# Z of the last two modes as column-group partials, channel sums of a third pair beside the last weights, and six tiles finished singly

## The chip, the cores and the metric

The kernel runs on one core of one Trainium2 chip. The metric is device time in microseconds for one execution, the median of three runs. All times below are microseconds unless marked otherwise; positions are counted from the start of the profiled span.

## The reference

Linear attention (batch 8, 8 heads, 576 rows, head size 64) feeds a Fourier mixing layer of width 512. Of the 576 rows' spectrum the first 64 modes are kept, and each mode has its own complex 512 x 512 matrix:

```python
q_p, k_p = (phi(q), phi(k))                      # phi(x) = elu(x) + 1
kv = np.einsum('bhsd,bhse->bhde', k_p, v)
...
x = (num / den) ...                              # (8, 576, 512)
X = np.fft.rfft(x, axis=1)                       # the first 64 modes: Xr, Xi
Yr = np.einsum('bmd,mde->bme', Xr, w_r) - np.einsum('bmd,mde->bme', Xi, w_i)
Yi = np.einsum('bmd,mde->bme', Xr, w_i) + np.einsum('bmd,mde->bme', Xi, w_r)
y = np.fft.irfft(Y, n=S, axis=1)
u = x + y
return u + np.maximum(u @ w_ch, 0.0)
```

The weights w_r and w_i are 64 x 512 x 512 each, in float32 in HBM, and are read once.

## The kernel before

**Stages.** First the attention of the 8 batches and the forward transform, while the first weights load. Then 32 mode pairs: `mode_pair(p)` multiplies two modes by their weights as they land (`product`, L498), copies the result off (`evacuate`), picks it apart into a bank `yt` (`picks`, L521), and does slots of other work (`work_slot`), with filler products (`keep_warm`, L485, into the bank `zl`) where PE would idle. Weights are loaded by POOL's DMA queue, two pairs of buffers deep. Rows of the output are made of x, the inverse transform of Y, and the relu of E0 (= x @ w_ch and early modes) plus the inverse transform of Z = Y @ w_ch. Early and middle modes are folded into x and E0 during the mode pairs.

**The last pair.** `last_pair` handles modes 62 and 63. The last eight modes (`Y8`, 128 rows of mode x part x batch, 16 a mode) are turned in two steps. `ahead_rows` does the first six (rows 0 to 95, `RA` = 96): transposes to `ya_ps`, products with w_ch to `za_ps`, and two copies on ACT into `ahead` (the tile `rows_ahead`). Then follow the channel sums of tile pairs 0 and 1 (`channels`, L932: an identity product that puts E0 into an accumulator) with the middle modes' Z behind them (`first_rows`, L1024, 64 rows of the array); mode 62's products; its picks; and mode 63's products (`y_last`, L583), piece by piece as the weights land in five pieces, with a filler behind some of them. `ahead_gathers` sends the 96 ahead rows to their places in `YZ_all` by two DMAs, one of SP and one of POOL, which wait for the third piece from the end.

**The tail.** When mode 63's Y is copied (L591), all four chunks of `Y8` are transposed (L1102) and multiplied by w_ch in two halves of 256 columns (L1108, into `zl` and `z1l`); ACT and DVE copy Y to `last_y`, ACT copies both halves of Z to `last_z`. Output rows come in 36 tiles of 128 rows, done as 18 pairs. Pairs 0 to 3 (batches 0 and 1) take Y and Z straight from `last_y` and `last_z`, by `lead_sb`, the inverse transform's rows in the order of `Y8`. Later pairs read `YZ_all`, so they need the gathers; the rows of modes 62 and 63 go there by four POOL DMAs (L1118), Z first. For each tile: channel sum, Z product (`add_inverse` with half 1), relu on ACT in place, Y product (half 0), add on DVE to x, store by SP. Tile 0 has its Y added ahead (`y0`, L1115) and is finished by one DVE operation; three more tiles are finished singly (`add_one`, L1130); from pair 2 on `finish` (L965) adds two tiles in one DVE operation and stores 512 KB.

**Order.** `pin` keeps the written order on each engine. So PE does pair n's sums and Z product, then pair n-1's Y product. Accumulators lie in eight banks, two for a pair, given out in turn (`acc_pools`); `declare_no_dep` tells the tile framework that two banks of one tile do not depend on each other.

Of the kernel before, what the change touches and what calls it, by code (L numbers as in the profile page):

```python
# [10 lines left out]
F32 = mybir.dt.float32  # L11
# [22 lines left out]
def kernel(  # L34
# [10 lines left out]
    nc = tc.nc  # L45
# [428 lines left out]
    def w_get(p: int):  # L474
# [5 lines left out]
        return w_in[p]  # L480

    def keep_warm(n: int, cols: int = D):

        for _ in range(n):
            pin(nc.tensor.matmul(last_ps[0][:, 0:cols], id16, wch16[:, 0, 0:cols]))  # L485

# [31 lines left out]
    def picks(kk: int, st, n: int):  # L518
        for ec in range(NDC):
            pin(  # L520
                nc.tensor.matmul(  # L521
                    yt_ps[:, ec, kk % 8 : kk % 8 + n, :].rearrange("p m n -> p (m n)"),
                    st[:, ec * 128 : ec * 128 + 128],
                    pick_sb[:, 0 : n * 2 * B],
                )
            )

    def mode_pair(p: int):
        nonlocal yt_ps
        w = w_get(p)  # L530
        if p % 4 == 0:
            yt_ps = psW.tile([128, NDC, 8, 2 * B], F32, tag="yt", bufs=1, name=f"yt{p // 4}")
        P = psW.tile([128, D], F32, tag="P", bufs=2, name=f"P{p}")
        for dc in range(NDW):
            product(P, xz[p % 2][:, dc].rearrange("p h n -> p (h n)"), 32, w, dc, NDW)
        if p + 1 < LAST:
            set_diagonal(p + 1)
        st = evacuate(p, P)
        work_slot(p, "mid")
        if p == LAST - 1:  # L540
            keep_warm(3)
        picks(2 * p, st, 2)
        if p % 4 == 3:
            kk = 2 * p + 1
            if kk < NF:
                pin(nc.vector.tensor_copy(out=YE_T[:, :, kk - 7 : kk + 1, :], in_=yt_ps))
# [8 lines left out]
    def last_pair():  # L555
        xl = ystage.tile([128, NDL, 2 * B], BF16, name="xl")
        for h in range(2):
            src = xt_v[:, (2 * h + 1) * NDC : (2 * h + 2) * NDC, :, :, LAST]
            pin(
                nc.vector.tensor_copy(  # L560
                    out=xl[:, h * NDC : h * NDC + NDC], in_=src.rearrange("p c t b -> p c (t b)")
                )
            )
        w = w_get(LAST)
        kk = NM - 2
        ahead_rows()
        work_slot(LAST, "start")
        P = psW.tile([128, D], F32, tag="P", bufs=2, name=f"P{kk}")
# [6 lines left out]
        pin(nc.vector.tensor_copy(out=Y8[:, :, NA, :], in_=yt_ps[:, :, NA, :]))  # L575
        ahead_gathers()
        keep_warm(4)
        y_last = psW.tile([128, NDC, 2 * B], F32, tag="P", bufs=2, name="y_last")
        for piece in PIECES:
            for dc in range(piece.start, piece.stop):  # L580
                for ec in range(NDC):
                    pin(
                        nc.tensor.matmul(  # L583
                            y_last[:, ec, :], w[:, NDL + dc, ec * 128 : ec * 128 + 128], xl[:, dc, :],
                            start=(dc == 0 and ec == 0), stop=(dc == NDL - 1), skip_group_check=True,
                        )
                    )
# [3 lines left out]
        nc.vector.tensor_copy(out=Y8[:, :, NL - 1, :], in_=y_last)  # L591

# [7 lines left out]
    PSUM = bass.MemoryType.PSUM  # L600
    psW = tc.alloc_tile_pool(name="psW", bufs=1, space=PSUM, side="left")
    psB = tc.alloc_tile_pool(name="psB", bufs=1, space=PSUM, side="right")

# [14 lines left out]
    def late_modes(g: int, ps):  # L618
# [7 lines left out]
        for h, yl in enumerate(YL):  # L626
            rows = mode_rows(ps)[:, h * (NDC // 2) : h * (NDC // 2) + NDC // 2]
            for d in range(2):
                pin(nc.vector.tensor_copy(out=yl[:, :, d, :, g, :], in_=rows))

# [56 lines left out]

    last_ps = []

# [181 lines left out]
    def fold_lead(t: int):  # L871
# [13 lines left out]
        pin(nc.scalar.copy(out=e, in_=acc))  # L885

    def add_inverse(n: int, half: int, tiles_of=(0, 1)):

# [35 lines left out]
    def channels(n: int, tiles_of=(0, 1)):  # L924
        if n not in accs:
            accs[n] = acc_pools[n % 4 // 2].tile([128, 2, D], F32, tag="acc", bufs=2, name=f"acc{n}")
        for i in tiles_of:
# [46 lines left out]

    last_ps.append(psW.tile([128, D], F32, tag="zl", bufs=1, name="zl0"))
    made: set = set()
# [15 lines left out]
    for b in range(B):  # L992
        work.append(lambda b=b: form_z(b))
        work.append(lambda b=b: form_y(b))
        if b < N_LEAD:
            work += [lambda t=t: fold_lead(t) for t in range(b * NJJ, b * NJJ + NJJ)]
    n_form = len(work) - n_fold
    first_fold, first_form = NF // 2 - 1, NE // 2 - 1
# [21 lines left out]
    def first_rows(n: int):  # L1020
        for i, t in enumerate(pairs[n]):
# [22 lines left out]
    def ahead_rows():  # L1044

        pin(nc.vector.tensor_copy(out=Y8[:, :, 0:NA, :], in_=yt_ps[:, :, 0:NA, :]))
        ya_ps = psW.tile([128, NDC, 128], F16, tag="P", bufs=2, name="ya_ps")
        za_ps = psW.tile([128, D], F32, tag="P", bufs=2, name="za_ps")
        for ec in range(NDC):
# [34 lines left out]
    for n in range(N_PRE):  # L1084
# [3 lines left out]

    last = [
        sW.tile([128, D], F16, tag="x16w", bufs=2, name="last_y"),  # L1090
        sW.tile([128, NDC, 128], F16, tag="xTw", bufs=2, name="last_z").rearrange("p c r -> p (c r)"),
    ]
    z1_ps = psW.tile([128, NDC, 8, 2 * B], F32, tag="yt", bufs=1, name="z1l")
    y_ps = [
        psW.tile([128, NDC, 128], F16, tag="P", bufs=2, name=f"ypl{h}")[:, 0 : NDC // 2] for h in range(2)
    ]
    y0 = psW.tile([128, D], F32, tag="P", bufs=2, name="y0l")
    last_ps.append(z1_ps.rearrange("p c m n -> p (c m n)"))
    hw = D // 2
    COLS = [slice(h * hw, h * hw + hw) for h in range(2)]  # L1100
    for ec in range(NDC):
        pin(nc.tensor.transpose(y_ps[ec // 2][:, ec % 2, :], rows[ec], id16))  # L1102
    pin(nc.scalar.copy(out=last[0][:, COLS[0]], in_=y_ps[0].rearrange("p c r -> p (c r)")))
    pin(nc.vector.tensor_copy(out=last[0][:, COLS[1]], in_=y_ps[1].rearrange("p c r -> p (c r)")))
    for h in range(2):
        for ec in range(NDC):
            pin(
                nc.tensor.matmul(  # L1108
                    last_ps[h][:, 0:hw], rows[ec], wch16[:, ec, COLS[h]],
                    start=(ec == 0), stop=(ec == NDC - 1),  # L1110
                )
            )
        pin(nc.scalar.copy(out=last[1][:, COLS[h]], in_=last_ps[h][:, 0:hw]))
    pin(nc.tensor.matmul(y0, lead_sb[0][:, rows_of(0)], last[0]))
    pin(nc.vector.tensor_tensor(out=x_of(0), in0=y0, in1=x_of(0), op=ALU.add))  # L1115
    for z in (1, 0):
        for h in range(2):
            nc.gpsimd.dma_start(out=late_at(h, RA, 128 - RA)[:, :, z, :], in_=last[z][RA:128])  # L1118
    psW.release()
    acc_pools.append(  # L1120
        tc.alloc_tile_pool(name="psT1", bufs=1, space=PSUM, side="left", reuse_waits="tile")
    )
# [17 lines left out]
    on_bank(  # L1140
        0, {0},
        nc.vector.scalar_tensor_tensor(
            out=x_of(0), in0=accs[0][:, 0], scalar=0.0, in1=x_of(0), op0=ALU.max, op1=ALU.add
        ),
    )
    store(0, 1)
# [12 lines left out]
    for n in range(4, len(pairs)):  # L1159
# [3 lines left out]
    finish(len(pairs) - 1)  # L1163
    acc_pools[1].release()
    acc_pools[0].release()

# [28 lines left out]
```

## Time and profile before

| | |
|---|---|
| median of 3 runs (lowest, highest) | 419.69 (419.50, 419.86) |
| the profiled execution | 419.94 |
| its span | 418.2 |
| PE / DVE / ACT / POOL busy | 71% / 57% / 37% / 15% of the span |
| weights' queue (POOL) | 81.53 MB |
| SP's queue | 10.90 MB |
| last piece of weights lands | 387.3 |
| first store issued | 391.0 |
| last store issued, landed | 413.0, 417.3 |

The span runs from the first to the last instruction; the profiled execution is 1.7 longer than it. In rows of the timeline the columns are start, duration (of the whole group, from the first start to the last end), engine, line, operation, output<-inputs, shapes and count, and in brackets the idle time before and what ended it. In a row of a stretch, each engine has its busy time and count, then come the granted clock of TensorE, the DMA share and GB/s. A row of DMA issues ends with the size of each and the time from issue to landing. Rows of the chain are start, duration, and the work that the end hung on.

### The profile page before, as it was taken

To read this page: it belongs to the slowest core of one execution; us is meant where nothing else is said; L and a number is where in the kernel's file an instruction comes from. 1 tells how busy PE (TensorE), PEld (TensorE's weight loads), DVE (VectorE), ACT (ScalarE), POOL (GpSimd) and SP (SyncE) were. 2 spreads that over 40 slices of the span, in tenths; PEclk is the share of its full clock that TensorE was granted. 3 is DMA by queue.
4 is the path that set the end of the run, shared out by engine and by line. 5 is a ranking of instruction groups with operands and counts; after the bars stand their busy time and mean duration, and the time that the engine had idled before them with its cause. 6 is when DMAs were issued, how large, how long until landed. Compare 5 with 4: busy or idle time off the path is not lost.

```text
span 418.2 us, 6982 instructions
## 1 busy us (share of the span) xinstructions
PE 295.0 (71%) x2890; PEld 158.9 (38%) x2890; DVE 240.2 (57%) x533; ACT 153.2 (37%) x226; POOL 61.3 (15%) x110
## 2 busy tenths in 40 slices
PE   0279999999674455444435676978796967998992
PEld 0167777777411222212122232333342422453431
DVE  4779879995437474455536453564454534522794
ACT  4667767954200001000000233334352522331682
POOL 6222222300020111111111111111111111130200
PEclk9999999989755655556665589999897988899997
DMA  8999999999999999999999999999999999998698
GB/s 216 212 212 214 211 219 205 222 215 220 212 215 218 213 221 212 216 217 216 218 216 215 219 212 216 218 215 217 216 215 218 215 215 219 215 210 172 210 401 344
DMA packets 16564, 92.86 MB, mean 222 GB/s; under 512 B 2069, under 2 KB 2790, under 8 KB 12374
## 3 DMA queue, kind: packets, MB, share of 16 engines
q0 software_dynamic: 12656, 81.53, 93.8%
q1 hardware_dynamic: 3878, 10.90, 6.9%
q8 instruction: 22, 0.36, 0.3%
q14 instruction: 8, 0.07, 0.0%
HBM read 163.66 MB, written 9.44 MB: 414 GB/s over the span
## 4 chain that ended last, share of the span: by engine, by line
DMA 55%; PE 25%; DVE 10%; ACT 3%; issue 3%; POOL 3%; ACTq 0%; POOLq 0%
DMA w<-in_moe_w_i_dram 52%; PE P L498 5%; PE kvp L258 5%; DVE x_main L965 4%; DMA k<-in_k_dram 3%; DVE x L294 3%; PE xf L417 2%; PE qTp L238 2%; PE xp L385 2%; POOL w L109 2%; PE num L156 1%; PE zl L485 1%; PE z L858 1%; ACT qT L245 1%; PE xf L422 1%
## 5 line engine op out<-in xcount | busy, mean ns | idle before, releaser
L498 PE MATMUL P<-w,xz 128*32 128x512 bf16 x496 | 49.2, 537 | 71.7 <-DMA w<-in_moe_w_i_dram 69.4
L109 POOL DMA_DIRECT2D w<-in_moe_w_r_dram x31 | 17.2, 553 | 247.9 <-PE P L498 246.2
L515 ACT CAST ys<-P 128x512 f16<-128x512 f32 x15 | 8.8, 586 | 118.1 <-PE P L498 112.3
L498 PEld LDWEIGHTS <-xz 128*32 128x32 bf16 x496 | 12.9, 117 | 93.8 <-DMA w<-in_moe_w_i_dram 77.3
L513 DVE CAST ys<-P 128x512 f16<-128x512 f32 x17 | 11.8, 692 | 58.0 <-PE P L498 58.0
L838 PE MATMUL eps<-wch,xTw 128*128 128x512 f16 x144 | 42.0, 420 | 0.0
L819 DVE TENSOR_TENSOR x_main<-ya,x_main 128x512 f32<-128x512 f32 x32 | 22.0, 689 | 20.5 <-PE ya L815 20.3
L821 ACT CAST x16w<-x_main 128x512 f16<-128x512 f32 x32 | 19.8, 618 | 37.1 <-DVE x_main L819 35.4
L258 PE MATMUL kvp<-vpad,ke 32*128 32x130 f16 x576 | 24.0, 265 | 8.5 <-ACT qT L245 8.5
L846 ACT CAST E<-eps 128x512 f16<-128x512 f32 (+1 forms) x40 | 21.2, 540 | 22.4 <-PE eps L838 22.4
L769 PE MATMUL nw<-kv_diag,qT 128*128 128x130 f16 (+1 forms) x160 | 24.6, 297 | 6.4 <-DVE x_tail L782 3.2
L258 PEld LDWEIGHTS <-ke 32*128 32x128 f16 x576 | 22.2, 117 | 10.0 <-issue 9.6
L508 DVE COPY xz<-xt_c 64x256 bf16<-64x256 bf16 x62 | 22.9, 369 | 2.2 <-PE P L498 1.4
L294 DVE TENSOR_TENSOR x<-num,rd 128x512 f16<-128x512 f32 x32 | 22.1, 691 | 1.1
L238 PE MATMUL qTp<-id,qe 128*128 128x128 f16 x144 | 15.2, 289 | 10.1 <-DVE qe L222 9.6
L769 PEld LDWEIGHTS <-qT 128*128 128x128 f16 (+1 forms) x160 | 14.5, 134 | 19.9 <-issue 11.4
L156 PE MATMUL num<-kv_sb,qT 64*128 64x65 f16 (+1 forms) x320 | 16.3, 219 | 5.7 <-DVE x L294 3.3
L245 ACT COPY qT<-qTp 128x1152 f16<-128x1152 f16 x16 | 19.6, 1293 | 2.0 <-PE qTp L238 1.5
L782 DVE TENSOR_TENSOR x_main<-nw,rd 128x256 f32<-128x256 f32 x32 | 11.2, 415 | 15.8 <-PE nw L769 15.8
L830 DVE COPY xTw<-xTp 128x512 f16<-128x512 f16 x36 | 15.0, 416 | 6.8 <-PE xTp L828 6.8
L838 PEld LDWEIGHTS <-xTw 128*128 128x128 f16 x144 | 13.7, 107 | 11.8 <-issue 4.7
L204 ACT ACTIVATE ke<-k 128x2304 f16<-128x2304 f16 x8 | 16.9, 2112 | 2.6 <-DMA k<-in_k_dram 2.6
(153 smaller groups left out, 525.2 us busy)
## 6 DMA issues: line engine op xcount, KB each, us to landing
w<-in_moe_w_r_dram POOLq DMA_DIRECT2D x31, 1024.0 KB, 12.5
w<-in_moe_w_i_dram POOLq DMA_DIRECT2D x31, 1024.0 KB, 16.8
out_dram<-x_main SPq DMA_DIRECT2D x14, 512.0 KB, 3.5
k<-in_k_dram POOLq DMA_DIRECT2D x8, 576.0 KB, 12.0
v<-in_v_dram POOLq DMA_DIRECT2D x8, 576.0 KB, 12.4
q<-in_q_dram POOLq DMA_DIRECT2D x7, 576.0 KB, 11.7
q<-in_q_dram SPq DMA_DIRECT2D x2, 576.0 KB, 4.4
w<-in_moe_w_r_dram POOLq DMA_DIRECT2D x2, 512.0 KB, 11.5
```

The costliest lines, as they stand in the source:

```text
L109: nc.gpsimd.dma_start(out=w_in[p][half::2], in_=two.rearrange("g (r dc) e -> (g r) dc e", dc=NDW))
L156: mm = nc.tensor.matmul(num[hpo][orow, c0 : c0 + 65], qT[rows, hpp, h2, cols], kv_sb[rows, hpp, h2, :])
L238: nc.tensor.transpose(qT_ps[:, j], phi["q", b][:, c, j].rearrange("p o d -> p (o d)"), id16,)
L245: nc.scalar.copy(out=qT[:, :, c * NJ : (c + 1) * NJ], in_=qT_ps.rearrange("p j x -> p x j"))
L258: nc.tensor.matmul(kv_ps[:, h2, 0:130], phi["k", b][r0 : r0 + 32, j // NJ, j % NJ].rearrange("p o d -> p (o d)"), vp[r0 : r0 + 32, :, j, 0 ...
L294: nc.vector.tensor_tensor(out=dst.rearrange("p (o c d) -> p o c d", o=2, c=4), in0=nv[:, :, :, 0:64], in1=rden.unsqueeze(3).broadcast_to([ ...
L498: nc.tensor.matmul(P[c : c + n, :], x, w[:, dc, :], start=(dc < NDC), stop=(dc >= n_dc - NDC), tile_position=(0, c), skip_group_check=True,)
L508: pin(nc.vector.tensor_copy(out=xz[p % 2][HALVES[h], :, h, :], in_=src))
L769: nc.tensor.matmul(num[c][orow, h2 * 130 : h2 * 130 + 130], qT[:, c, h2, rows_of(jj, BASE[b % 2])], kv_diag[:, b, c, h2].rearrange("p o n ...
L819: pin(nc.vector.tensor_tensor(out=x, in0=acc, in1=x, op=ALU.add))
L838: nc.tensor.matmul(e_ps, xT[:, c, :], wch16[:, c, :], start=(c == 0), stop=(c == NDC - 1))
L846: pin(nc.scalar.copy(out=dst, in_=e_ps[:, cols]))
```

## The change

- **Banks.** One tile `sums` of two banks takes the place of `yt` and `zl`; `in_sums` pins and declares the two banks apart. `P` moves to a pool of its own, which is released in `last_pair`, so that pair 2's accumulator takes its place there; pair 3's takes `sums`.
- **Beside the last weights.** `first_rows` also adds the ahead rows' Z to pairs 0 and 1 (96 rows of the array). Two of the four fillers ahead of `y_last` go, and the two channel sums of pair 2 (`N_PRE`) come. `y_last` goes to `sums`.
- **Gathers.** Both ahead gathers are POOL's.
- **Z of the last two modes.** Only rows 96 to 127 are done. Each of the four chunks' product with w_ch goes to its own 32 columns of the array and its own 32 partitions, unsummed; one copy on ACT makes `zq`. For pairs 0 and 1 the sum over the chunks is made by the inverse product itself, with `lead4`, which holds those 32 rows of `lead_sb` four times (made early, by `spread_rows`, a new item of work behind batch 0's folds). For the others `pick_sb` sums the chunks and DVE copies the result into rows 96 to 127 of `ahead`, whose Y rows come from DVE as well. The four late gathers read from there, Y first.
- **Tiles.** Tile 0's own path (`y0`) goes. All six tiles of pairs 0 to 2 are finished singly; pair 3's sums are made tile by tile.

The diff, cut to its core:

```diff
         ahead_gathers()
-        keep_warm(4)
-        y_last = psW.tile([128, NDC, 2 * B], F32, tag="P", bufs=2, name="y_last")
+        psP.release()
+        acc_pools.append(
+            tc.alloc_tile_pool(name="psT2", bufs=1, space=PSUM, side="left", reuse_waits="tile")
+        )
+        keep_warm(2)
+        channels(N_PRE)
+        y_last = yt_ps[:, :, NL - 1, :]
...
+    def spread_rows():
+
+        r = slice(RA, 128)
+        r_ps = bank("lead4_ps")
+        for q in range(4):
+            pin(
+                nc.tensor.matmul(
+                    r_ps[32 * q : 32 * q + 32, :], id16[r, r], lead_sb[0][r, 0:512],
+                    tile_position=(RA, 32 * q), skip_group_check=True,
+                )
+            )
...
+        pin(nc.scalar.copy(out=lead4[0], in_=r_ps))
...
-                if n < 2 * N_LEAD:
-                    mm(i, orow, lead_sb[b][:, sel_rows], last[half])
+                if n < N_PRE and half == 1:
+                    mm(i, orow, lead4[0][:, sel_rows], zq)
+                elif n < 2 * N_LEAD:
+                    mm(i, orow, lead_sb[b][:, sel_rows], ahead[:, half, :])
...
     def first_rows(n: int):
         for i, t in enumerate(pairs[n]):
             on_bank(...)
+            on_bank(
+                n, {i},
+                nc.tensor.matmul(
+                    accs[n][:, i], lead_sb[0][0:RA, rows_of(t, BASE[0])], ahead[0:RA, 1, :],
+                    start=False, stop=False, skip_group_check=True,
+                ),
+            )
...
-        for h, eng in enumerate((nc.sync, nc.gpsimd)):
-            g = eng.dma_start(
+        for h in range(2):
+            g = nc.gpsimd.dma_start(
...
+    z_ps, y_ps = sums[:, 1], sums[:, 0].rearrange("p (c r) -> p c r", c=NDC)
     for ec in range(NDC):
-        pin(nc.tensor.transpose(y_ps[ec // 2][:, ec % 2, :], rows[ec], id16))
...
+        in_sums(
+            1,
+            nc.tensor.matmul(
+                z_ps[32 * ec : 32 * ec + 32, :], rows[ec][:, r_new], wch16[:, ec, :],
+                tile_position=(0, 32 * ec), skip_group_check=True,
+            ),
+            apart=False,
+        )
+    for ec in range(NDC):
+        in_sums(
+            0,
+            nc.tensor.matmul(
+                y_ps[r_new, ec, :], rows[ec][:, r_new], id16, tile_position=(0, RA), skip_group_check=True
+            ),
+        )
+    in_sums(1, nc.scalar.copy(out=zq, in_=z_ps))
+    in_sums(
+        0, nc.vector.tensor_copy(out=ahead[r_new, 0, :], in_=y_ps[r_new].rearrange("p c r -> p (c r)"))
     )
...
-    add_inverse(0, 1, (1, 0))
...
+    add_inverse(0, 1, (0,))
+    relu(0, 0)
+    z_new = sums[r_new, 1]
+    in_sums(1, nc.tensor.matmul(z_new, pick_sb, zq, tile_position=(0, RA), skip_group_check=True))
+    in_sums(1, nc.vector.tensor_copy(out=ahead[r_new, 1, :], in_=z_new))
+    for z in (0, 1):
+        for h in range(2):
+            nc.gpsimd.dma_start(out=late_at(h, RA, 128 - RA)[:, :, z, :], in_=ahead[r_new, z, :])
+    add_inverse(0, 1, (1,))
     relu(0, 1)
...
-    singles = [(0, 1), (1, 0), (1, 1)]
-    soon = [(2, (0,)), (2, (1,)), (3, (0, 1))]
+    singles = [(n, i) for n in range(3) for i in range(2)]
+    soon = [None, (2, 0), (2, 1), (3, 0), (3, 1)]
     for n, i in singles:
         add_inverse(n, 0, (i,))
         if soon:
-            sums_of(*soon.pop(0))
+            nxt = soon.pop(0)
+            if nxt:
+                sums_next(*nxt)
         add_one(n, i)
-    finish(2)
```

In the built program PE has pair 4's two Z products, which read `YZ_all`, ahead of pair 3's two Y products; so it was before, too.

More of the change, by code (lines that the diff above doesn't have):

```diff
@@ L480, in w_get, with in_sums @@
         return w_in[p]
+    on_sums: list = [[], []]
+    def in_sums(bank: int, ins, apart: bool = True):
+        pin(ins)
+        for other in on_sums[1 - bank] if apart else ():
+            tc.declare_no_dep(ins.ins, other.ins, reason="the other bank of the sums")
+        on_sums[bank].append(ins)
     def keep_warm(n: int, cols: int = D):
         for _ in range(n):
-            pin(nc.tensor.matmul(last_ps[0][:, 0:cols], id16, wch16[:, 0, 0:cols]))
+            in_sums(1, nc.tensor.matmul(last_ps[0][:, 0:cols], id16, wch16[:, 0, 0:cols]))
     work: list = []
@@ L519, in picks @@
         for ec in range(NDC):
-            pin(
+            in_sums(
+                0,
                 nc.tensor.matmul(
@@ L524, in picks @@
                     pick_sb[:, 0 : n * 2 * B],
-                )
+                ),
             )
@@ L531, in mode_pair @@
         if p % 4 == 0:
-            yt_ps = psW.tile([128, NDC, 8, 2 * B], F32, tag="yt", bufs=1, name=f"yt{p // 4}")
-        P = psW.tile([128, D], F32, tag="P", bufs=2, name=f"P{p}")
+            yt_ps = sums[:, 0].rearrange("p (c m n) -> p c m n", c=NDC, m=8)
+        P = psP.tile([128, D], F32, tag="P", bufs=2, name=f"P{p}")
         for dc in range(NDW):
@@ L545, in mode_pair @@
             if kk < NF:
-                pin(nc.vector.tensor_copy(out=YE_T[:, :, kk - 7 : kk + 1, :], in_=yt_ps))
+                in_sums(0, nc.vector.tensor_copy(out=YE_T[:, :, kk - 7 : kk + 1, :], in_=yt_ps))
             else:
@@ L567, in last_pair @@
         work_slot(LAST, "start")
-        P = psW.tile([128, D], F32, tag="P", bufs=2, name=f"P{kk}")
+        P = psP.tile([128, D], F32, tag="P", bufs=2, name=f"P{kk}")
         for dc in range(NDL):
@@ L574, in last_pair @@
         picks(kk, st, 1)
-        pin(nc.vector.tensor_copy(out=Y8[:, :, NA, :], in_=yt_ps[:, :, NA, :]))
+        in_sums(0, nc.vector.tensor_copy(out=Y8[:, :, NA, :], in_=yt_ps[:, :, NA, :]))
         ahead_gathers()
-        keep_warm(4)
-        y_last = psW.tile([128, NDC, 2 * B], F32, tag="P", bufs=2, name="y_last")
+        psP.release()
[5 more added lines that the diff above has]
+        y_last = yt_ps[:, :, NL - 1, :]
         for piece in PIECES:
@@ L581, in last_pair @@
                 for ec in range(NDC):
-                    pin(
+                    in_sums(
+                        0,
                         nc.tensor.matmul(
@@ L585, in last_pair @@
                             start=(dc == 0 and ec == 0), stop=(dc == NDL - 1), skip_group_check=True,
-                        )
+                        ),
                     )
@@ L590, in last_pair @@
                 keep_warm(1, D // 2)
-        nc.vector.tensor_copy(out=Y8[:, :, NL - 1, :], in_=y_last)
+        in_sums(0, nc.vector.tensor_copy(out=Y8[:, :, NL - 1, :], in_=y_last))
     while pending:
@@ L601 @@
     psW = tc.alloc_tile_pool(name="psW", bufs=1, space=PSUM, side="left")
+    sums = psW.tile([128, 2, D], F32, tag="sums", bufs=1, name="sums")
+    psP = tc.alloc_tile_pool(name="psP", bufs=1, space=PSUM, side="left")
     psB = tc.alloc_tile_pool(name="psB", bufs=1, space=PSUM, side="right")
@@ L628, in late_modes @@
             for d in range(2):
-                pin(nc.vector.tensor_copy(out=yl[:, :, d, :, g, :], in_=rows))
+                in_sums(0, nc.vector.tensor_copy(out=yl[:, :, d, :, g, :], in_=rows))
     def late_rows(ec: int, b: int):
@@ L686, in bank @@
         return psB.tile(list(shape), dtype, tag="bank", bufs=4, name=name)
-    last_ps = []
+    last_ps = [sums[:, 1]]
     sel = sW.tile([128, 1 + N_LEAD, 128], F16, tag="rows", bufs=1, name="row_sel")
@@ L885, in fold_lead @@
         pin(nc.scalar.copy(out=e, in_=acc))
+    lead4: list = []
+    def spread_rows():
[8 more added lines that the diff above has]
+            )
+        lead4.append(
+            sW.tile([128, NDC, 128], F16, tag="xTw", bufs=2, name="lead4").rearrange("p c r -> p (c r)")
+        )
+        pin(nc.scalar.copy(out=lead4[0], in_=r_ps))
     def add_inverse(n: int, half: int, tiles_of=(0, 1)):
@@ L925, in channels @@
         if n not in accs:
-            accs[n] = acc_pools[n % 4 // 2].tile([128, 2, D], F32, tag="acc", bufs=2, name=f"acc{n}")
+            pool, tag, bufs = ((acc_pools[0], "acc", 2), (acc_pools[-1], "acc", 1), (psW, "sums", 1))[
+                max(n % 4 - 1, 0)
+            ]
+            accs[n] = pool.tile([128, 2, D], F32, tag=tag, bufs=bufs, name=f"acc{n}")
         for i in tiles_of:
@@ L973, in spread @@
         return range(n_items * step // steps, n_items * (step + 1) // steps)
-    last_ps.append(psW.tile([128, D], F32, tag="zl", bufs=1, name="zl0"))
     made: set = set()
@@ L996 @@
             work += [lambda t=t: fold_lead(t) for t in range(b * NJJ, b * NJJ + NJJ)]
+        if b == 0:
+            work.append(spread_rows)
     n_form = len(work) - n_fold
@@ L1044, in ahead_rows @@
     def ahead_rows():
-        pin(nc.vector.tensor_copy(out=Y8[:, :, 0:NA, :], in_=yt_ps[:, :, 0:NA, :]))
-        ya_ps = psW.tile([128, NDC, 128], F16, tag="P", bufs=2, name="ya_ps")
-        za_ps = psW.tile([128, D], F32, tag="P", bufs=2, name="za_ps")
+        in_sums(0, nc.vector.tensor_copy(out=Y8[:, :, 0:NA, :], in_=yt_ps[:, :, 0:NA, :]))
+        ya_ps = psP.tile([128, NDC, 128], F16, tag="P", bufs=2, name="ya_ps")
+        za_ps = psP.tile([128, D], F32, tag="P", bufs=2, name="za_ps")
         for ec in range(NDC):
@@ L1086 @@
     last_pair()
[L1089 to L1098, printed above, removed]
@@ L1099 @@
-    hw = D // 2
-    COLS = [slice(h * hw, h * hw + hw) for h in range(2)]
-    for ec in range(NDC):
-        pin(nc.tensor.transpose(y_ps[ec // 2][:, ec % 2, :], rows[ec], id16))
[L1103 to L1121, printed above, removed]
+    r_new = slice(RA, 128)
+    z_ps, y_ps = sums[:, 1], sums[:, 0].rearrange("p (c r) -> p c r", c=NDC)
@@ new lines @@
+    zq = ystage.tile([128, D], F16, tag="ystage", bufs=2, name="zq")
+    for ec in range(NDC):
+        in_sums(
[3 more added lines that the diff above has]
+                tile_position=(0, 32 * ec), skip_group_check=True,
+            ),
+            apart=False,
+        )
+    for ec in range(NDC):
+        in_sums(
+            0,
+            nc.tensor.matmul(
+                y_ps[r_new, ec, :], rows[ec][:, r_new], id16, tile_position=(0, RA), skip_group_check=True
+            ),
+        )
@@ L1122 @@
+    in_sums(1, nc.scalar.copy(out=zq, in_=z_ps))
+    in_sums(
+        0, nc.vector.tensor_copy(out=ahead[r_new, 0, :], in_=y_ps[r_new].rearrange("p c r -> p (c r)"))
     )
@@ L1137, in sums_of @@
             relu(n, i)
-    add_inverse(0, 1, (1, 0))
[L1140 to L1146, printed above, removed]
+    add_inverse(0, 1, (0,))
[7 more added lines that the diff above has]
+    add_inverse(0, 1, (1,))
     relu(0, 1)
@@ L1150, with sums_next @@
         relu(1, i)
-    singles = [(0, 1), (1, 0), (1, 1)]
-    soon = [(2, (0,)), (2, (1,)), (3, (0, 1))]
+    def sums_next(n: int, i: int):
+        add_inverse(n, 1, (i,)) if n == N_PRE else sums_of(n, (i,))
+        if n == N_PRE:
+            relu(n, i)
+    singles = [(n, i) for n in range(3) for i in range(2)]
+    soon = [None, (2, 0), (2, 1), (3, 0), (3, 1)]
     for n, i in singles:
@@ L1164 @@
     acc_pools[1].release()
+    psW.release()
     acc_pools[0].release()
```

## The prediction

> **What bounds the kernel now.** I read the chain that ended last first, then PE in order of time around the last weights, then short stretches of the tail, then single DMA issues with their landings. The chain:
>
> ```profile
> 372.36 13.64 DMA w<-in_moe_w_i_dram
> ...
> 387.64 0.24 DVE Y L591
> ...
> 389.23 0.38 ACT last_z L1113
> ...
> 395.03 1.04 DVE x_main L965
> ...
> 411.76 1.23 DVE x_main L965
> ```
>
> Up to 386 the weights bound it. The last piece, issued at 378.07, lands 9.2 us later, at 387.3. The Y copy (L591) runs from 387.64 for 0.22; its end, 387.87, I call T. From T to the span's end, 418.2, the tail is 30.3 us. PE just before T:
>
> ```profile
> 381.68 0.59 PE L932 MATMUL acc<-E,id 128*128 128x512 f16 x2
> 382.21 0.62 PE L1024 MATMUL acc<-YZ_all,inv_sb 64*128 64x512 f16 x2
> 382.76 0.66 PE L498 MATMUL P<-w,xt_c 128*32 128x512 bf16 x8
> ...
> 384.44 0.26 PE L521 MATMUL yt<-pick_sb,ys 128*128 128x16 f16 x4
> 384.55 1.02 PE L485 MATMUL zl<-wch,id 128*128 128x512 f16 x4
> 385.49 0.34 PE L583 MATMUL y_last<-xl,w 128*128 128x16 bf16 x8
> 386.04 0.36 PE L583 MATMUL y_last<-xl,w 128*128 128x16 bf16 x8 [0.21 <-DMA w<-in_moe_w_i_dram]
> ```
>
> Two things are to be seen. PE is hardly ahead of the weights: it waits 0.2 to 0.3 us for a piece. And a change of shape costs: a 512-column product takes 0.38 and its successor of the same shape starts 0.215 later (four in 1.02), but L1024, of 64 rows, starts 382.21 - 381.68 - 0.215 = 0.31 after the product ahead of it; L498 starts 0.31 after the second L1024 (which followed the first by 0.24). So a change costs 0.09 extra.
>
> In the tail the chain names DVE, but the stretches name the store DMAs:
>
> ```profile
> 391.00:396.00 5.00, 5.00 (x26) 2.11 (x25) 4.18 (x5) 4.03 (x8) 1.25 (x3) 1.00 0.75 255
> 396.00:413.00 17.00, 14.89 (x86) 4.82 (x86) 16.98 (x15) 12.91 (x13) 0.00 (x0) 1.00 1.01 402
> ```
>
> The last two columns are the DMA share and GB/s. From 396 on the 16 engines are full at 402 GB/s, so a 512 KB store takes 1.30 us, while DVE offers one every 1.18 to 1.2. The landings show the queue grow (stores of 396.29 and 413.02):
>
> ```profile
> out_dram<-x_main SPq DMA_DIRECT2D x1, 512.0 KB, 2.7
> out_dram<-x_main SPq DMA_DIRECT2D x1, 512.0 KB, 4.3
> ```
>
> The first (pair 3) lands at 399.0 = T + 11.14; fourteen more at 1.307 end at T + 29.43 = 417.30, 0.9 before the span's end. So the end is set by when pair 3 lands, and by T.
>
> **The change: ahead of T.** `first_rows` gets a 96-row product behind each 64-row one: four more, and the order on PE alternates. The trace has no 96-row product; from below it costs 0.215 (same shape goes on), from above 0.31 (a change each time). I take 0.31: 96 rows don't fit the 64-row shape, and both neighbouring rows, 64 to 128 and back, cost it. Pair 0 then takes 0.215 + 5 x 0.31 = 1.77 to L498, not 1.08: +0.69. (Its first 96-row product needs the second ahead copy of ACT, 382.46, and is there at 382.52: no extra wait.) L498 starts at 383.45; its weights have been there since 382.3. Pair 1 takes 1.67, not 1.09: +0.58. The picks start at 385.70, not 384.44; their operand, DVE's copy of P, ends at 384.83 and hides. Two keep-warm products become two channel sums of pair 2: same size, no cost. y_last starts at 386.68, not 385.49; all pieces but the last two have landed, so PE runs through: 32 small products at 0.025, two fills of 0.215, one of 0.11 and a last latency of 0.17 are 1.51, to 388.19, not 387.60. That is T + 0.57: T' = 388.44. At the lower price nothing moves, since PE would start y_last at 385.93 and still wait for weights.
>
> The Trainium skill, TensorEngine Tiling (Array Packing), Key Properties, says that changing the tiling mode, though not the tile, drains the engine, and under Available Configurations row tiling is for 64 or 32 rows. By that a 96-row product between 64-row ones is a change both ways, the upper price; by a reading in which 96 rows share the mode, T' = T. The trace agrees on 64 against 128 rows (0.31 against 0.215); 96 no run here shows yet.
>
> **Ahead of that, nothing.** `spread_rows` (four small products, one ACT copy of about 0.59) pushes one item more into the last slot ahead of mode pair 30, some 0.3 on PE; PE idles 0.60 before pair 30's products at 377.82, waiting for weights. If that cover were gone, 0.3 would reach T. The bank `sums` replaces two single-buffered ones: no new wait with the banks declared apart.
>
> **From T' to the first store.** Removed: eight 256-column Z products, two half copies on ACT, y0 and its add. Before, T to the first store is 391.00 - 387.87 = 3.14. Now (offsets from T'): four Z products in four column groups run together, as the first four of L498 do (0.44): 0.06 to 0.50. ACT's copy zq of 512 columns, 0.59 as in L862: to 1.13. First lead4 product 1.18 to 1.55, relu (0.58, L1126) to 2.17. Behind that product PE has z_new (a change of shape, 0.31) and three more sums; the Y product runs 2.44 to 2.82, DVE's add 2.85 to 3.54. The store waits for two more semaphores on SP at 0.06: 3.69. So +0.55 against before. DVE then adds singles every 0.65: issues at 4.22, 4.86, 5.51, 6.16, 6.81, the sixth landing near 10.0 (3.2 each, as single 2 to 4 before). Before, those six tiles had landed at 9.93: the singles make good the late start and no more.
>
> **The gathers.** Both ahead gathers now sit on POOL (SP, which loses one, was idle until the first store): 387.49 to about 388.7, hidden, needed at pair 4. Then Y rows (after DVE's copy, 0.69 as L513, ending 1.46; POOL starts 0.29 after its release, as L1118 after ACT) at 1.75 and 2.35, 0.6 each as in L1118, then Z rows at 2.95 and 3.55: Y goes first now, and Z was first before. Z's copy of z_new ends at 2.63, in time. L1118 landed 2.7 to 3.2 after issue, so Z is there at 6.25 to 6.75; before, at T + 5.3. PE reaches pair 4's Z product at 5.84 and waits to about 6.55. Queued behind it on PE are pair 3's two Y products, and behind them DVE's add and SP's store: Y products at +0.34 and +0.25, end +0.38, add 1.22, so pair 3 is stored at 8.79 and lands 2.72 later, 11.51; pair 4 at about 12.8.
>
> **Sum.** Pair 3 lands at T' + 11.3 (Z early; the store queue itself allows no less) to 11.8, before T + 11.14; with 14 x 1.307 behind it the tail is 0.15 to 0.7 longer, I take 0.42. With 0.57 that is +0.99: span 419.2, profiled execution 419.94 + 0.99 = 420.93. The median of before is 0.25 below its profiled execution: 419.69 + 0.99 = 420.7.
>
> **Rivals.**
> - PE's 96-row products cost 0.215 or less: T' = T, only the tail's 0.42 is left, 420.1. For it: no row shows one. Chance 0.20.
> - Faster: the DMA share in 391 to 396 is 0.75, and 0.60 and 0.54 in the two halves of the last of these microseconds. Six singles feed this hole. Once saturated, 36 tiles need 23.5 us; the hole is worth 0.5. It decides if T' is below 388.1 and Z lands before T' + 5.8: 419.2. Against: the Z rows are issued fourth, behind 0.6 us each. Chance 0.06.
> - Z rows land later, at T' + 7.2 or more, as they share the engines with the first stores: 0.65 more, 421.3. Before, the one issued after the first store took the longest, 3.2. Chance 0.18. The Trainium skill, SBUF — State Buffer, SBUF: two separate sides, has GpSimd's descriptor writing locked out while DVE runs a copy in a two-port mode, which would add z_new's 0.69 here. In this trace L1118's issues stay at 0.6 beside DVE's adds, which are no copies; so it's open.
> - The column groups don't run together, so Z takes 4 x 0.215: +0.65, 421.3. Against: L498. Chance 0.06.
>
> **Numbers.** The forecast has 0.50, with its own range 420.2 to 421.2. About 0.2%, 0.84 us, is what a measurement of this kernel can tell from no change; 420.53 is that bound. Of the forecast three quarters lie above it: with the two late cases, slower 0.61; same is its other quarter and the first rival, 0.34; faster, most of its rival, 0.05. The range runs from 419.6, near the faster case, to 421.7, the late ones.
>
> **What would show it.** Right: PE's y_last products run without a DMA wait and end near 388.2; 96-row products 0.31 apart; PE waits for a DMA ahead of pair 4's first product, with pair 3's add on DVE behind it; pair 3's store near 397.2; DMA share 1.0 from then on. Wrong: a wait for weights just ahead of the last y_last products (T unchanged), or DVE without a gap between single 6 and pair 3.

## The result, and the profile after

The changed kernel takes 421.65 (median of nine executions, 420.28 to 423.66); the kernel before takes 419.63 (nine on the same chip, 419.29 to 419.86). The ratio is 1.0056, with a 95% interval of 1.0045 to 1.0066: slower, in the direction forecast, but by 2.0 where 1.0 was forecast. It also scatters over 3.4, where the kernel before scatters over 0.6. One thing is needed to read its profile: the profiled execution, 420.28 with a span of 418.6, is the fastest of the nine, so most of the loss is not in its trace. Runs e1 and e4 below, with profiled executions of 423.19 and 421.87, have it.

The chain that ended last, in the profile after:

```profile
359.55 17.47 DMA w<-in_moe_w_i_dram
391.43 3.02 DMA YZ_all<-rows_ahead
396.59 1.17 DVE x_main L1005
...
412.19 1.23 DVE x_main L1005
```

The last weights and the Y copy are gone from it: the chain enters the tail through the fourth late gather. PE in order of time, from mode pair 30's products to Z:

```profile
377.06 1.05 PE L506 MATMUL P<-w,xz 128*32 128x512 bf16 x16 [0.41 <-DMA w<-in_moe_w_i_dram]
...
381.45 0.40 PE L1065 MATMUL acc<-YZ_all,inv_sb 64*128 64x512 f16 x1
381.78 0.41 PE L1072 MATMUL acc<-rows_ahead,lead_sb 96*128 96x512 f16 x1
382.12 0.40 PE L1065 MATMUL acc<-YZ_all,inv_sb 64*128 64x512 f16 x1
...
386.15 0.55 PE L598 MATMUL sums<-xl,w 128*128 128x16 bf16 x16
...
387.40 0.24 PE L598 MATMUL sums<-xl,w 128*128 128x16 bf16 x4
387.96 0.40 PE L1143 MATMUL sums<-wch,Y 128*32 128x512 f16 x4
```

Two things are to be seen. The 96-row products (L1072) start 0.34 after the 64-row ones and the other way round, and y_last (now L598) runs without a wait for weights: PE, not the weights, now ends last. The last weights land at 386.92 and T is 387.91: 0.99 behind them, not 0.57. The four column groups of Z take 0.40 together.

The same stretches of the tail, and the stores of pair 3 (396.70) and of the last pair (413.44):

```profile
391.00:396.00 5.00, 4.69 (x21) 1.79 (x21) 4.00 (x7) 3.75 (x7) 1.02 (x2) 1.00 0.78 257
396.00:413.00 17.00, 15.32 (x90) 4.98 (x87) 16.98 (x15) 13.12 (x13) 0.00 (x0) 1.00 0.99 391
```

```profile
out_dram<-x_main SPq DMA_DIRECT2D x1, 512.0 KB, 2.6
out_dram<-x_main SPq DMA_DIRECT2D x1, 512.0 KB, 4.2
```

The first store goes out at T + 3.69 (before 3.14), pair 3 lands at T + 11.43 (before 11.14), the last one at T + 29.76 (before 29.44). Ahead of the second of pair 4's Z products PE waits for the last gather, which lands at T + 6.53:

```profile
394.49 0.37 PE L927 MATMUL acc<-YZ_all,inv_sb 64*128 64x512 f16 x1 [0.31 <-DMA YZ_all<-rows_ahead]
```

The 17 us behind 396 move 391 GB/s and not 402, since the hole in the stores (a DMA share of 0.57 at 395 to 396 before, 0.58 at 397 to 398 after) has moved into them. From T to the span's end it is 30.7, before 30.3.

### The profile page after: what moved, and what is told of

Read it like the earlier page. It is cut to its first block, busy times and chain, and to the rows that moved or that the text cites. A ratio compares the mean times of both kernels' runs of the same rounds, so it can differ in the third digit from the quotient of the medians.

```text
span 418.6 us, 6996 instructions
## 1 busy us (share of the span) xinstructions
PE 288.7 (69%) x2893; PEld 154.8 (37%) x2893; DVE 240.4 (57%) x534; ACT 153.4 (37%) x226; POOL 61.7 (15%) x111
## 4 chain that ended last, share of the span: by engine, by line
DMA 61%; PE 15%; DVE 11%; ACT 5%; issue 4%; POOL 3%; ACTq 0%; POOLq 0%
DMA w<-in_moe_w_i_dram 53%; DMA k<-in_k_dram 7%; PE P L506 6%; DVE x_main L1005 4%; DVE x L294 2%; ACT qT L245 2%; PE kvp L258 2%; POOL w L109 2%; PE xp L385 1%; ACT ke L204 1%; PE xf L417 1%; ACT kv_sb L270 1%; PE num L156 1%; DMA YZ_all<-rows_ahead 1%; DVE rd L291 1%
## 5 line engine op out<-in xcount | busy, mean ns | idle before, releaser
L258 PE MATMUL kvp<-vpad,ke 32*128 32x130 f16 x576 | 22.3, 251 | 8.5 <-ACT qT L245 8.5
L258 PEld LDWEIGHTS <-ke 32*128 32x128 f16 x576 | 20.6, 110 | 9.8 <-issue 9.2
L238 PE MATMUL qTp<-id,qe 128*128 128x128 f16 x144 | 13.3, 265 | 10.8 <-DVE qe L222 9.6
```

The lines of the kernel that those rows point to most:

```text
L258: nc.tensor.matmul(kv_ps[:, h2, 0:130], phi["k", b][r0 : r0 + 32, j // NJ, j % NJ].rearrange("p o d -> p (o d)"), vp[r0 : r0 + 32, :, j, 0 ...
```

## The experiments

Throughout, "P30" is the start of mode pair 30's first product, and it is *late* by its distance from the landing of its weights: 0.04 where PE waits for them. In the profiled executions:

| kernel | its time | half clock, 345 to 362 | P30 late | P30 to y_last | T less last landing | T to end |
|---|---|---|---|---|---|---|
| before | 419.94 | 352.0, 6.8 long | 0.04 | 7.67 | 0.57 | 30.3 |
| after | 420.28 | none | 0.04 | 9.10 | 0.99 | 30.7 |
| e1 | 423.19 | 351.0, 10.2 | 2.78 | 9.09 | 3.45 | 30.6 |
| e2 | 421.99 | 351.9, 6.8 | 0.96 | 9.11 | 2.46 | 31.0 |
| e3 | 422.53 | 350.3, 10.2 | 1.99 | 8.60 | 2.34 | 30.6 |
| e4 | 421.87 | 352.2, 6.8 | 1.06 | 9.11 | 2.49 | 30.7 |
| e5 | 421.25 | 350.2, 10.2 | 0.89 | 9.10 | 1.82 | 30.5 |
| e6 | 421.86 | 347.7, 13.7 | 3.51 | 7.59 | 2.17 | 30.3 |
| e7 | 419.57 | 351.7, 6.8 | 1.23 | 7.59 | 0.67 | 30.3 |
| e8 | 420.54 | 351.7, 6.8 | 0.04 | 8.60 | 0.57 | 30.6 |
| e9 | 419.75 | 352.3, 6.8 | 0.04 | 7.60 | 0.57 | 30.6 |
| e10 | 420.15 | none | 0.04 | 8.60 | 0.57 | 30.8 |
| e11 | 420.79 | 354.6, 3.4 | 0.58 | 9.11 | 1.54 | 30.6 |
| e12 | 419.83 | none | 0.04 | 8.60 | 0.57 | 30.7 |
| e13 | 420.10 | none | 0.04 | 8.60 | 0.56 | 30.8 |
| e14 | 419.26 | none | 0.04 | 8.04 | 0.57 | 30.3 |

Every row follows one sum: T is the later of *last landing + 0.57* and *P30 + (P30 to y_last, unhindered) + 1.76*, where 1.76 is the time from y_last's first product to the end of the Y copy when no weights are waited for. The unhindered stretch is 7.59 without the 96-row products, 8.60 with them grouped and 9.10 with them in turn. For e4, 378.58 + 9.11 + 1.76 = 389.45, which is its T.

**e1, the changed kernel again.** No edit.

> The changed kernel as it is, profiled again. Its first profiled execution took 420.28 with a span of 418.6, but the median of its nine executions is 421.65. Theory A, PE late ahead of T and the Z rows late in the tail: the same picture again, T' about 0.4 to 0.6 after the weights would allow and a tail of 29.8, and a time within 0.4 of 420.3. Theory B, a delay that falls into most executions and not into the first profiled one: a time of 421.4 to 423.7, and this profile shows a place where 1 to 3 us are lost that the first one doesn't have, in the weights' stream (last piece later than 387.3) or in the tail (longer than 29.8 from T').

422.49 (421.57 to 423.19), ratio 1.0063 (1.0042 to 1.0084). Its profile, at 423.19, is 3.25 above that of before, and T takes 3.02 of it: the loss stands ahead of T.

**e2, one ahead gather on SP.**

```diff
-        for h in range(2):
-            g = nc.gpsimd.dma_start(
+        for h, eng in enumerate((nc.sync, nc.gpsimd)):
+            g = eng.dma_start(
```

> The changed kernel with one of the two ahead gathers back on SP, as before. Theory A: Z rows are issued 0.0 to 0.6 earlier only if POOL's queue was what held them; the trace shows POOL free in time, so no change over 0.2. Theory B with the place in POOL's queue (six DMAs written there in a row, next to the stores): the loss of 1 to 2 us goes, about 420.2, and the executions scatter less.

422.37 (421.99 to 423.37), ratio 1.0069 (1.0051 to 1.0088). POOL's queue is not the cause: P30 is 0.96 late here too. (The longer time from T to the end, 31.0, is taken up under e13.)

**e3, the two 64-row products first, then the two 96-row ones.**

```diff
         on_bank(n, {i}, ... 64 rows)
+    for i, t in enumerate(pairs[n]):
         on_bank(n, {i}, ... 96 rows)
```

> The changed kernel with the two 64-row products of a pair first and its two 96-row products behind them, so that the array changes shape two times less in a pair. Theory A: each change costs 0.12 (0.337 against 0.215), so PE is 0.44 earlier at y_last, PE waits for the last weights again, T' comes 0.35 to 0.45 earlier, and so does the end. Theory B: 0.4 at most, and the scatter stays.

421.97 (421.33 to 422.53), ratio 1.0051 (1.0035 to 1.0068). P30 to y_last falls from 9.10 to 8.60, as two changes of shape fewer for each tile pair should make it, but P30 itself was late by 1.99.

**e4, Z's late gathers first.**

```diff
-    for z in (0, 1):
+    for z in (1, 0):
```

> The changed kernel with the late gathers of Z ahead of those of Y. Theory A: Z's issue is bound by DVE's copy of z_new plus 0.29, so Z goes out 0.4 to 0.6 earlier, its two products of pair 4 and pair 3's add by up to 0.6, and the end by 0.2 to 0.4, as the store queue takes over. Y rows go out later by 1.2, and are still in time for pair 4's Y product, which stands behind its relu. Theory B: no change over 0.4, and the scatter stays.

422.4 (421.87 to 422.82), ratio 1.0061 (1.0046 to 1.0077). The order of the gathers brings nothing: Z's go out at T + 2.95 in either order, since POOL waits for DVE's copy of z_new. But this trace, at 421.87, is near the changed kernel's median (421.65) and shows what an execution of that length has. Its order ahead of T is the changed kernel's. First e4:

```profile
360.63 0.46 PE L885 MATMUL yp<-id,YL 128*128 128x128 f16 x4
361.83 0.37 PE L894 MATMUL yb<-YZ_all,inv_sb 64*128 64x512 f16 x1 [0.74 <-DVE YZ_all L886]
...
375.90 2.75 PE L493 MATMUL sums<-wch,id 128*128 128x512 f16 x12
378.58 1.05 PE L506 MATMUL P<-w,xz 128*32 128x512 bf16 x16
```

and before:

```profile
359.62 1.05 PE L498 MATMUL P<-w,xz 128*32 128x512 bf16 x16
360.60 0.40 PE L877 MATMUL yb<-YZ_all,inv_sb 64*128 64x512 f16 x1
...
374.47 2.75 PE L485 MATMUL zl<-wch,id 128*128 128x512 f16 x12
377.82 0.40 PE L498 MATMUL P<-w,xz 128*32 128x512 bf16 x4 [0.60 <-DMA w<-in_moe_w_i_dram]
```

The new item shifts the list of work by one. The transposes of a Y (`form_y`, L885) moved from the end of mode pair 27 into the middle of pair 28, right ahead of the fold that reads them. So PE waits 0.74 for DVE's copy there, where before it began the fold at once; spread_rows itself took another 0.5, at half clock, ahead of pair 28. Both kernels had the same stretch of half clock, 6.8 long. At the end PE comes to P30 straight from the fillers, without a wait: 1.06 late, where before it had 0.60 to spare.

**e5, spread_rows without an item**: it stands behind pair 29, in place of two of the twelve fillers.

```diff
+        if p == LAST - 2:
+            spread_rows()
-        keep_warm(FILL.get(p, 0))
+        keep_warm(FILL.get(p, 0) - (2 if p == LAST - 2 else 0))
...
-        if b == 0:
-            work.append(spread_rows)
```

> The changed kernel, but the spread of lead4 is no item of the list of work: it is called at the end of mode pair 29, in the place of two of that slot's twelve fillers, so that every other item lies in the slot in which it was before the change. Theory C (new): the item pushes batch 1's Y rows from the slot ahead of mode pair 28 to the one behind its products, where the next item waits 0.73 for DVE's copy of them, and adds its own work; PE, which had 0.6 to spare at mode pair 30, is 1.0 to 2.8 late there, by the granted clock in the microseconds 351 to 361. Then here PE waits for weights again ahead of pair 30, T' is about 388.3, the scatter goes, and the time is 420.2 to 420.7. Theory A alone (nothing ahead of the last pair): unchanged, 422.

420.65 (420.26 to 421.44), ratio 1.0030 (1.0020 to 1.0040). Where the item stood was worth 1.1 to 1.4 of the loss (1.0056 and 1.0063 less 1.0030, of 419.6).

**e6, the kernel before with the item alone**, its product unused.

```diff
+        if b == 0:
+            work.append(spread_rows)
```

> The kernel before with nothing but the new item of work, whose result is not used. Theory C: PE's products of mode pair 30 start 1.0 to 2.8 after their weights, and as this kernel's last pair and tail have 0.3 of slack there, the time is 420.4 to 422, with a scatter of 1 to 2. Theory A: as before, 419.7.

420.2 (419.66 to 421.86), ratio 1.0018 (1.0005 to 1.0031). The scatter is there too. The profile fell on the longest execution: P30 3.51 late, T 2.17 behind the last landing and not 0.57 + 3.51 = 4.1. Without the 96-row products part of the lateness is still hidden.

**e7, the kernel before with an item that does nothing.**

```diff
+        if b == 0:
+            work.append(lambda: None)
```

> The kernel before with an item of work in the same place that does nothing: the shift of the items by one, and no work added. Theory C, if the shift alone does it (the 0.73 wait for DVE's copy): late by 0.7 to 1.5 at pair 29, by 0.1 to 0.5 at pair 30, so 419.7 to 420.3. If it needs the item's own work on PE as well (0.5): as before.

419.77 (419.57 to 420.81), ratio 1.0010 (1.0001 to 1.0020). The shift alone makes P30 1.23 late, and the kernel before hides all of that but 0.1. So the shift is the larger part of the lateness, and its price depends on what stands behind P30.

The rows of the mode pairs' products tell the shift from the clock. First pair 28 to pair 30 in e7, then in e5, where the items lie as in the kernel before:

```profile
359.25 1.05 PE L498 MATMUL P<-w,xz 128*32 128x512 bf16 x16
369.61 1.05 PE L498 MATMUL P<-w,xz 128*32 128x512 bf16 x16
378.18 1.05 PE L498 MATMUL P<-w,xz 128*32 128x512 bf16 x16
```

```profile
360.64 1.05 PE L506 MATMUL P<-w,xz 128*32 128x512 bf16 x16
369.86 1.05 PE L506 MATMUL P<-w,xz 128*32 128x512 bf16 x16
378.17 1.05 PE L506 MATMUL P<-w,xz 128*32 128x512 bf16 x16
```

None of these products waits for weights, so the distances are PE's own: 18.93 with the shift, 17.53 without, and 18.93 to 18.96 in each of e1 to e4, e6 and e11 too. The shift thus costs 1.40, 1.14 of it ahead of pair 29, whatever the clock did before. What varies is where pair 28 starts, and it goes with the length of the half clock: 0.04 behind its weights where there is no half clock (after, e10, e12 to e14), 1.2 with 3.4 of it (e11), 1.6 to 2.0 with 6.8, 2.8 to 3.2 with 10.2 and 4.0 with 13.7 (e6).

**e8, e5 with e3's grouping and e4's order.**

> e5 with the 64-row and 96-row products grouped and the late gathers of Z first. Theory C with A: T' 0.4 earlier than in e5 (387.9) and pair 3's landing another 0.2 to 0.4 earlier: 419.4 to 420.0, the same as the kernel before within 0.2%, or faster by at most 0.3.

420.39 (420.02 to 420.95), ratio 1.0021 (1.0012 to 1.0030).

**e9, e5 without the 96-row products.**

```diff
-            on_bank(n, {i}, nc.tensor.matmul(accs[n][:, i], lead_sb[0][0:RA, ...], ahead[0:RA, 1, :], ...))
```

> The kernel with spread_rows written out behind mode pair 29, without the 96-row products of first_rows (it leaves out what the ahead rows add to Z of the tile pairs 0 and 1; every other step is there). If the 96-row products take the slack behind mode pair 30: from the start of pair 30's products to the first y_last product 7.6 us in place of 9.10, so that about 1.1 us of lateness at pair 30 is hidden again and T follows the last weights; what is left is the tail's 0.3: 419.8 to 420.2. If the lateness ahead is all and the 96-row products cost nothing beside it: as with them, 420.65.

419.99 (419.72 to 421.21), ratio 1.0011 (1.0001 to 1.0020). The first y_last products run, and then wait again for weights:

```profile
385.06 0.35 PE L600 MATMUL sums<-xl,w 128*128 128x16 bf16 x8
385.65 0.36 PE L600 MATMUL sums<-xl,w 128*128 128x16 bf16 x8 [0.24 <-DMA w<-in_moe_w_i_dram]
```

P30 to y_last is 7.60, T is the last landing + 0.57, and what is left is the tail. Beside e5 the four products cost 0.8 (1.0030 less 1.0011), more than the 0.42 that they take in the profile after: by the sum above they also take the cover of whatever lateness there is.

**e10, e8 with nine more keep-warm products**, around mode pairs 26 and 27. This asks where the scatter comes from. TensorE's granted clock has stretches of one half, each a multiple of 3.4 long, but for the one that the program's end cuts off. PE alone, in windows of that length that end where a stretch begins or ends (the columns are PE's busy time, the granted clock, the DMA share and GB/s). Before:

```profile
348.61:352.03 3.42, 1.87 (x20) 1.00 1.03 220
352.03:355.44 3.41, 2.90 (x10) 0.50 1.04 221
355.44:358.85 3.41, 3.41 (x12) 0.50 0.99 211
```

e1:

```profile
347.53:350.95 3.42, 1.31 (x20) 1.00 0.99 211
350.95:354.36 3.41, 2.81 (x10) 0.50 1.06 226
354.36:357.77 3.41, 3.41 (x12) 0.50 1.04 221
357.77:361.19 3.42, 3.42 (x12) 0.50 1.06 225
```

In the windows ahead of the half clock PE had idled for 45% of the time and more. Then come three windows at half clock in e1, two in before. Where the windows lie against the program differs from execution to execution: the profile after has no half clock here, its stretch lies at 337. The edit fills PE's idle time at 347 to 351:

```diff
-        if p == LAST - 1:
+        if p in (LAST - 4, LAST - 1):
             keep_warm(3)
         picks(2 * p, st, 2)
...
+        if p == LAST - 4:
+            keep_warm(3)
         work_slot(p, "end")
...
-    FILL = {..., 27: 7, 28: 10, 29: 12, 30: 2}
+    FILL = {..., 26: 3, 27: 7, 28: 10, 29: 12, 30: 2}
```

> The version with spread_rows written out behind mode pair 29, the 96-row products grouped and the late gathers of Z first, and besides nine keep-warm products on TensorE around mode pairs 26 and 27 (three at the end of pair 26, three ahead of the picks of pair 27, three behind its late modes). If the stretch of half clock at 350 to 361 us comes from PE's idle time in 344 to 351 and makes PE late at mode pair 30: no half clock there, pair 30 late by 0.1 or less, 419.8 to 420.0 with less scatter. If the lateness is a matter of the order of the work alone: as without the nine, 420.4, or later by their 9 x 0.215 us.

420.19 (419.82 to 420.52), ratio 1.0013 (1.0004 to 1.0023), 0.2 more than expected. First the two windows of the clock, then P30, both of e10:

```profile
348.39:351.81 3.42, 3.22 (x29) 1.00 1.05 225
351.81:355.22 3.41, 2.69 (x17) 1.00 1.00 211
```

```profile
377.18 1.05 PE L506 MATMUL P<-w,xz 128*32 128x512 bf16 x16 [1.33 <-DMA w<-in_moe_w_i_dram]
```

There is no half clock, and PE reaches P30 1.33 ahead of the weights.

**e11, the changed kernel with the same nine products and nothing else.**

> The changed kernel with the same nine keep-warm products and nothing else. If the clock makes the lateness at mode pair 30: full clock at 350 to 361, pair 30 late by 0 to 1, 420.3 to 421.0, with less scatter than the changed kernel has. If the shifted items alone make it: 421.7 to 422.4 as before the edit.

420.46 (420.04 to 422.84), ratio 1.0023 (1.0009 to 1.0037). Nine products that compute nothing take back 1.4 to 1.7 of the loss (1.0056 and 1.0063 less 1.0023). Eight of the ten executions lie within 420.04 to 420.79, two above; in the profiled one the stretch is 3.4 long and P30 0.58 late.

**e12, e10 with pair 3's Y products ahead of pair 4's Z products.**

```diff
         channels(n)
+        if n == 4:
+            finish(n - 1)
         rectified(n)
-        finish(n - 1)
+        if n > 4:
+            finish(n - 1)
```

> The version of the nine keep-warm products with pair 3's Y products put ahead of pair 4's Z products on PE, so that pair 3's add and store don't stand behind the wait for the gathered Z rows. If the store queue's late refill at pair 3 sets the tail: pair 3 stored 0.2 to 0.5 earlier, tail 30.45 or less, 419.6 to 419.8. If the queue has enough without it: tail 30.65, as without the edit.

420.04 (419.79 to 420.36), ratio 1.0007 (0.9997 to 1.0016): not to be told from the kernel before. Pair 3 is stored 1.15 earlier (T + 7.82), yet it lands at T + 11.64, as in e10 (11.61), behind the singles in the queue, and DVE's idle time moves from ahead of pair 3 to ahead of pair 4:

```profile
393.92 1.21 DVE L1009 TENSOR_TENSOR x_main<-acc,x_main 128x1024 f32<-128x1024 f32 x1
396.26 3.61 DVE L1009 TENSOR_TENSOR x_main<-acc,x_main 128x1024 f32<-128x1024 f32 x3 [1.13 <-PE acc L931]
```

**e13, e12 with Z's late gathers issued by SP.**

```diff
-    for z in (1, 0):
-        for h in range(2):
-            nc.gpsimd.dma_start(...)
+    for z, queue in ((0, nc.gpsimd), (1, nc.sync)):
+        for h in range(2):
+            queue.dma_start(...)
```

> The version with nine keep-warm products and pair 3's Y products first, with the two late gathers of Z issued by SP in place of POOL, which then issues Y's two alone. If the gathers' line on POOL holds pair 4's add (there the fourth landed at T + 8.3, and DVE stood idle for 1.13 ahead of that add): all four land by T + 6.5, DVE's gap is 0.3 or less, pair 4 is stored 0.8 to 1.1 earlier and the tail is 29.6 to 30.0: 419.0 to 419.4, below the kernel before. If the store engines are full by then anyway: tail 30.5, as without the edit, 420.0.

420.1 (419.78 to 420.57), ratio 1.0013 (1.0004 to 1.0022), and not the 419.0 to 419.4 expected if the gathers' line on POOL were what holds pair 4. DVE's gap ahead of pair 4 shrinks from 1.13 to 0.67 only, and SP's two issues take 1.47 in front of the first store, which goes out at T + 4.22 where it was T + 3.68:

```profile
390.13 1.47 SPq L1186 DMA_DIRECT2D YZ_all<-rows_ahead  x2
391.64 0.92 SPq L991 DMA_DIRECT2D out_dram<-x_main  x2
395.76 3.61 DVE L1009 TENSOR_TENSOR x_main<-acc,x_main 128x1024 f32<-128x1024 f32 x3 [0.67 <-PE acc L931]
```

Yet the last store goes out at T + 25.14 and lands at T + 29.53, where e12 has 25.60 and 29.75. In this execution 0.22 is gained up to the last landing and lost behind it: the span ends 1.28 after that landing, in e12 0.91 after. At the end SP goes through a list of closing waits. In e12 the one that the last store's landing ends is the last of the list; in e13 six more follow it, one every 0.06. In e2, which also has a gather on SP, seven follow, and the span ends 1.35 after the last landing.

**e14, the kernel before with the nine keep-warm products.**

> The kernel before, with the same nine keep-warm products and nothing else. If they only take away lateness at mode pair 30 that the kernel before hides anyway: no half clock at 350 to 361, pair 30 late by 0.04 as before, ratio 1.000 within 0.001. If a full clock there wins time in itself: 0.5 or more faster, 419.2 or less.

419.52 (419.26 to 419.75), ratio 0.9999 (0.9990 to 1.0008). P30 in its profile:

```profile
376.85 1.05 PE L498 MATMUL P<-w,xz 128*32 128x512 bf16 x16 [1.31 <-DMA w<-in_moe_w_i_dram]
```

The clock is full here too and PE 1.31 ahead, and it is worth nothing. So the fillers win no time in themselves; they take away lateness that the kernel before hides and the changed kernel does not.

## Why the prediction was right or wrong

**The step that failed is "Ahead of that, nothing".** It priced spread_rows at 0.3 on PE, hidden by the 0.60 that PE idles ahead of P30, and gave 0.3 as the cost if that cover were gone. In e4, the trace near the median, P30 is 1.06 late, so PE lost 1.6 to 1.7 against before; in e1 it is 2.78 late, a loss of 3.3 to 3.4. Three things were missed. The item's own time is 0.5 to 0.6 at half clock. The step costed one item more in the last slot, which was about right (pair 29 to pair 30 takes 8.57 in e7, 8.31 in e5), but not the shift of the other items, though the list in the kernel gives their order: form_y now stands right ahead of the fold that reads it, a wait of 0.74, and the shift as a whole costs 1.40 (e7 has it without the product, and is 1.23 late). And the step took the cover from one execution, while the stretch of half clock ahead of it lies differently in each (e1, e6 against after; e10 and e11 for the cause).

The measured 421.65 still lies just below the range's upper end, 421.7. That is luck: the upper end was put there for two late cases in the tail, and neither came.

**"96 rows" at the upper price: right.** The change of shape was put at 0.31 and is 0.34; y_last starts 1.4 to 1.5 later behind P30 (forecast 1.19), and with PE on time T came 0.42 later for it (forecast 0.57). The rival in which 96 rows cost nothing is out. What was not seen is that the same products use up the slack behind P30: the sum T = max(last landing + 0.57, P30 + ...) could be worked out from rows of the trace before, and in the changed kernel it makes any lateness at P30 pass into T one for one. So the price of the lateness hung on the other step: e7's 1.23 is nearly hidden in the kernel before, and 1.06 in e4 is not hidden at all. By the ratios the item alone costs 0.8 in the kernel before (e6), the 96-row products and the tail without the item 1.3 (e5), and both together 2.3 to 2.6.

The Trainium skill, TensorEngine Tiling (Array Packing), Key Properties, has a change of tiling mode drain the engine, and by its Available Configurations 96 rows are no row tile. The trace agrees: 64 to 96 rows and back cost 0.34 each, while two 96-row products in a row (e3) are 0.62 for both.

**The tail: right.** +0.42 was forecast, within 0.15 to 0.7. It is 0.32 in the last landing, and in the time from T to the end 0.2 to 0.5 in the profiled tails (0.7 in e2, with its longer closing waits). First store +3.69, exactly as forecast; late gathers at +1.71 and +2.94 (forecast 1.75 and 2.95); the sixth single lands at +10.03 (10.0), pair 3 at +11.43 (11.51). The column groups run together. The late-Z rival is out, too: the last Z gather lands at T + 6.53, within the forecast's 6.25 to 6.75 and short of the rival's 7.2. POOL's issues stay at 0.6 (four in 2.40), also beside DVE's copy of z_new. So the lock-out that the Trainium skill, SBUF — State Buffer, SBUF: two separate sides, tells of for a two-port mode is not seen beside this copy, which reads PSUM. The rival of a filled store hole did not come: the hole in the stores (0.57 of the DMA share at 395 to 396 before) is at 397 to 398 after (0.58). In e12 it is gone (0.93 or more in every microsecond from 392 to 401), in e13 too (1.01 or more from 393 on). The last stores land at T + 29.75 and T + 29.53 there, against 29.76 after, so filling the hole brought 0.2 at most, where the rival gave it 0.5.

Why the tail is longer is shown in part. The late first store does not explain it alone: in e13 that store goes out later still, at T + 4.22, and yet the last one lands at T + 29.53, 0.1 behind before, where the other profiled tails of the changed kernel have 29.6 to 29.9. So DVE's wait for the gathered Z rows, 1.13 in e12 and 0.67 in e13, looks worth about 0.2, from one execution of each. The remaining 0.1 stays open, since no run took the first store's delay of 0.55 away. Nor does a run tell on what condition the clock is halved: see below.

## What to carry to other kernels

An item put into a list of work costs more than its own instructions: look at which producer it pushes right up against its consumer, and price each wait that comes of it. Before work is put on an engine that has some slack left, write down the slack as a sum from the last common start, since two changes that each fit into it may not fit together. Where an engine's clock can halve, a gap seen in one execution is no cover, and a few products that compute nothing may be worth as much as a reordering (1.4 to 1.7 in e11, 1.1 to 1.4 in e5), but only if the lateness that they prevent is not hidden already (e11 against e14).

## What the runs showed of the hardware

- **Half clock comes in windows of 3.4, free of the program.** The Trainium skill, TensorE: Matmul & The Clock Gate, Part 1, has a free-running window of 3.4 us, a clock of one half or full, and re-throttling after an idle window. Length, phase and the two clocks agree with the traces. "Idle" is less than it says: PE was 38% to 55% busy in the windows ahead of the half clock in before (1.87 of 3.42), e1 (1.31 of 3.42) and e4 (1.86 of 3.41). The busy time in the profile doesn't settle the condition, though: in e11 a window with 1.83 of 3.42 was followed by full clock, and one with 2.48 of 3.41 by half.
- **How long it stays is open, too.** In before PE was busy for 2.90 of 3.41 in the first window at half clock, and one more at half followed; after that one, with 3.41 of 3.41, came full clock. In e1 a window of 2.81 was followed by one with 3.41 of 3.41 and still a third at half, 10.2 in all.
- **A change of array rows costs about 0.12**: 0.34 from start to start against 0.215, whether from 64 to 96 rows or back.
- **Two DMA issues of small rows on SP took 1.47** (e13), longer than POOL's two (about 1.2), so SP was no free place for them. With them the wait for the last store also stood earlier among SP's closing waits, and the end came 0.37 later behind its landing (1.28 against 0.91 in e12).
